# Wide operands at multiples of 128 bytes, and one DRAM tensor of x for each pair of batches

## The chip, the cores and the metric

The kernel runs on one core of one Trainium2 chip. The metric is the time of one execution on the device, in microseconds (us), as the median of several runs; lower is better.

## The reference

Inputs are q, k and v of shape [8 batches, 8 heads, 576, 64] and four weight matrices, all fp32. An attention with two sparse masks is followed by a mixer of two MLPs. Cut to what matters:

```python
scores = np.matmul(q, k.transpose(0, 1, 3, 2)) / np.sqrt(64)
rel = pos[:, None] - pos[None, :]
mask_local = (rel >= 0) & (rel < 32)                       # heads 0 to 3
mask_strided = (rel >= 0) & (pos[None, :] % 32 == pos[:, None] % 32)   # heads 4 to 7
attn = softmax(np.where(mask, scores, -1e9))
x = np.matmul(attn, v)                     # heads side by side: [8, 576, 512]
xt = x.transpose(0, 2, 1)                  # [8, 512, 576]
h = np.maximum(xt @ w_tok1, 0) @ w_tok2    # 576 -> 256 -> 576
u = x + h.transpose(0, 2, 1)
out = u + np.maximum(u @ w_ch1, 0) @ w_ch2 # 512 -> 1536 -> 512
```

## The kernel before

**Number format.** Each fp32 operand of the MLPs is split into a high part of type float32r and the rest. Three matmuls (high x high, high x rest, rest x high) then stand for one. So weights have two copies (w1h and w1l, t1h and t1l, and so on), and activations too: xh and xlo, hh and hl, uh and ul, gh and gl.

**Attention.** It comes in three forms.
- *Local heads.* `local_unit` (L132) takes a pair of batches p, a pair of heads hp, and n chunks of 128 rows from chunk c0 on, out of the 2 x 576 = 1152 rows of the two batches laid end to end (nine chunks). It is a generator: each `yield` ends a stage (loads of lq, lk and lv; scores L145; transposes L163; values L173). It leaves its result in the tile lx and stores that to DRAM. A unit whose rows lie in one batch leaves in one store (L200). Batches are 4.5 chunks long, so a unit of chunks 3 to 5 straddles the two batches; it leaves in six stores of 64 rows each (L209).
- *Strided heads, batches 0 and 1.* `strided_pe` (L221) does them on TensorE: scores L233, transposes L245, values L257, stores L271. It loads eq, ek and ev (L216 to L218). Those of batch 1 run inside the MLP of batch 0, as two "lanes" (generators over the groups of rows in GS).
- *Strided heads, batches 2 to 7.* `strided` (L278) does them without TensorE: products on GpSimd (POOL, L312 and L335), sums on VectorE (DVE, L317 and L340). Its operands q, k, v and the result are tiles "sa" that share three buffers: the load of the next batch's v goes into the buffer that held this batch's result, once that has been stored. The result leaves in four stores, one for each head (L344).

**x.** The attention's result goes by way of DRAM. Before, each batch has two DRAM tensors of [576, 256]: local heads (called xl in the profile, `xd[0]`) and strided heads (xs, `xd[1]`). `load_x` (L347) reads one half of the columns of a batch back into the tile x ([128, 5 chunks, 512]) in three loads: four whole chunks (L350), and the last 64 rows twice, one copy in each half of the partitions (L352).

**Token MLP.** `tok1` (L354) splits each of the five chunks of x (cast on ScalarE, ACT, L362; rest on DVE, L365 or L368) and multiplies it with t1 (L380). `tok2` (L400) adds x, transposed on TensorE (L404), and the second product (L408, weights operand h, moving operand t2) in PSUM, and gives u. `tok2_tail` (L411, matmuls L417, weights operand t2, moving operand h) does the last 64 rows of a batch; these are kept in DRAM (`ud`) for a ninth, short pass over all batches.

**Channel MLP.** `mlp` (L515) runs over 12 blocks fc of 128 hidden features. `up_proj(fc)` is twelve matmuls of 128x512 into h (L532, weights w1, moving operand u), then a ReLU on ACT (L535) and the rest gl on DVE (L536). `down_proj(fc)` is twelve matmuls into four accumulators (L545, weights w2, moving operand g). The order is up 0, up 1, then up fc+2 and down fc in turn. After each block stands a *step* `done()`; the 24 steps of a batch are numbered 0 to 23, and `at(i, f)` puts work of other parts into step i. So TensorE always has work of the channel MLP of batch b, and the attention and the token MLP of later batches lie between its blocks:

- step 0: `tok2_tail` of batch b;
- steps 12 and 13 (b = 0 and 1) or 11 and 11 (later): `load_half` issues the loads of the local and the strided half of x of batch b + 1;
- steps 15 to 19 or 14 to 19: one chunk of `tok1` of batch b + 1 each; steps 20 to 23: its `tok2`;
- steps 1 to 12 of batch 0 (with a last call at 13): the lanes of batch 1's strided heads; steps 0 to 15 of batch 0: splitting of weights (`do_pieces`, L82 to L112);
- the table UNITS gives the steps of the stages of the local units of later batches; `some_strided` spreads the GpSimd form over the steps from 16 of batch 0 on.

**Order.** On TensorE, VectorE, ScalarE and GpSimd the instructions run in the order in which the code writes them (`manual_schedule`). All DMAs that matter here are issued by SyncE (SP), one queue, in an order that the scheduler sets from its own simulated timeline; an issue that has to wait (for its data or a free buffer) holds up those behind it.

**Places in SBUF.** Tiles are placed one after the other. The weights come first, then a small constant tile "below" (a bias for L96; [128, 16] fp32, so 64 bytes a partition, of which one column is used, L439), then x, h, xh, xlo, uh, ul, gh, gl, ot and others. The sizes of all of these, except "below", are multiples of 128 bytes. Tiles of the later local units are placed from the other end.

Of the kernel before, what the change touches and what calls it, by code (L numbers as in the profile page):

```python
# [10 lines left out]
F32 = mybir.dt.float32  # L11
# [8 lines left out]
B, H, S, D = 8, 8, 576, 64  # L20
HL = 4
ST = 32
DM = H * D
DT = 256
DF = 1536
P = 128
# [7 lines left out]
NSB = 2  # L34
# [3 lines left out]
NSC = 5  # L38
# [14 lines left out]
def attn_mixer_kernel(ctx, tc, qT, kT, vw, qs, ks, vs, qsT, ksT, vsP, mask, mask2, w1, w2, wt1, wt2, outT):  # L53
    nc = tc.nc

    const = ctx.enter_context(tc.tile_pool(name="const", bufs=1))
    dram = ctx.enter_context(tc.tile_pool(name="dram", bufs=1, space=bass.MemoryType.DRAM))
# [18 lines left out]

    ud = [dram.tile([TAIL, DM], F32, name=f"u{b}") for b in range(B)]

    xd = [[dram.tile([S, HL * D], F32, name=f"x{m}{b}") for b in range(B)] for m in "ls"]


    def convert(stage, srcs, n):  # L82
# [49 lines left out]
    def local_unit(pool, ps_t, p, hp, c0, n, into=None, single=()):  # L132
# [9 lines left out]
        for t in range(4 * n):  # L142
            c, a = divmod(t, 4)
# [26 lines left out]
        for t in range(4 * n):  # L170
            c, a = divmod(t, 4)
# [17 lines left out]
        if nd:  # L189
            x = x_t[:, nd].rearrange("p j d -> p (j d)")  # L190
            for r in range(2):
                nc.sync.dma_start(out=into[64 * r:64 * r + 64, NSC - 1, cs], in_=x[:64])
            nc.sync.dma_start(out=xd[0][1][:64, cs], in_=x[64:])
            return
        xa, xb = xd[0][2 * p], xd[0][2 * p + 1]
        s0 = P * c0
        if s0 >= S or s0 + P * n <= S:
            x = xa if s0 < S else xb
            s0 %= S
            nc.sync.dma_start(  # L200
                out=x[s0:s0 + P * n, cs].rearrange("(c p) d -> p c d", p=P), in_=x_t[:, :n].rearrange("p c j d -> p c (j d)"))
        else:

            for c in range(n):
                for r in range(0, P, 64):
                    t = s0 + P * c + r
                    x = xa if t < S else xb
                    t %= S
                    nc.sync.dma_start(out=x[t:t + 64, cs], in_=x_t[r:r + 64, c].rearrange("p j d -> p (j d)"))  # L209


    def strided_load(pool, b, hp):
# [8 lines left out]
    def strided_pe(pool, ps_t, b, hp, j, gs, loaded, outs):  # L221
        js = slice(64 * j, 64 * j + 64)
        q_t, k_t, v_t = loaded
        n = len(gs)
# [41 lines left out]
            nc.vector.tensor_scalar_mul(x_t[:r, nf, j], av[:r, D * nf:D * nf + D], z_t[:r, nf:n])  # L266
        if j == 1:

            to = xd[1][b][:, P * hp:P * hp + P].rearrange("(j r) d -> r j d", r=ST)
            for i, g in enumerate(gs):  # L270
                nc.sync.dma_start(out=to[RG * g:RG * g + rows[i] // NJ], in_=x_t[:rows[i], i].rearrange("p j d -> p (j d)"))  # L271
        yield
# [5 lines left out]
    def strided(pool, b):  # L278
# [62 lines left out]

        yield from rows(av, av_sum)
        for h in range(HL):
            nc.sync.dma_start(out=xd[1][b][:, D * h:D * h + D].rearrange("(j r) c -> r j c", r=ST), in_=o_t[ST * h:ST * h + ST])  # L344


    def load_x(x_t, b, half):  # L347
        cs = slice(HL * D * half, HL * D * half + HL * D)
        src = xd[half][b]
        nc.sync.dma_start(out=x_t[:, :NSC - 1, cs], in_=src[:P * (NSC - 1)].rearrange("(c p) d -> p c d", p=P))  # L350
        for r in range(2):
            nc.sync.dma_start(out=x_t[64 * r:64 * r + 64, NSC - 1, cs], in_=src[P * (NSC - 1):])  # L352

    def tok1(pool, ps_t, x_t, h, cs):  # L354

# [34 lines left out]
    def new_h(pool):  # L390
        return [[pool.tile([P, DM], F32R, name=f"h{k}{m}", bufs=1) for k in "hl"] for m in range(2)]
# [44 lines left out]
    rests = [stage.tile([P, DM], U32, name=f"w_rest{i}", bufs=1) for i in range(2)]  # L436
    for t in rests:
        nc.gpsimd.memset(t, 0)
    below = const.tile([P, 16], F32, name="below")[:, :1]  # L439
    nc.gpsimd.memset(below, -15.5 / 32)  # L440
    xp = ctx.enter_context(tc.tile_pool(name="xp", bufs=2))
    up0 = ctx.enter_context(tc.tile_pool(name="up0", bufs=1))
# [24 lines left out]
    with tc.tile_pool(name="first", bufs=2) as first, \  # L467
# [22 lines left out]
        run(*loc[:2], *st[:4])  # L490
        load_t1()
        run(*loc[2:], *st[4:])
        load_x(x_t, 0, 1)
        run(tok1(xp, ps_m, x_t, h, slice(0, HL * D)))
        load_t2()
        u = [tok2(up0, ps_m, x_t, h, cc) for cc in (0, 1)]
# [134 lines left out]
    for b in range(B):  # L631
        after = {}

        def at(i, f, *args):
            after.setdefault(i, []).append(lambda: f(*args))

        def load_next(b):
            x_t = xp.tile([P, NSC, DM], F32, name="x", bufs=1)
            x_next.update(x=x_t, h=new_h(xp), u=[])
            x_next["tok1"] = tok1(xp, ps_t, x_t, x_next["h"], slice(0, DM))  # L640

        def load_half(b, half):
            assert half == 0 or turn["batch"] > b or b < NSB, (b, turn)
            load_x(x_next["x"], b, half)

        def do_tok1():
            next(x_next["tok1"], None)
# [6 lines left out]

        at(0, tok2_tail, ps_t, x_t, h, b)
        if b + 1 < B:

            local, stride, steps = (12, 13, (15, 16, 17, 18, 19, 19)) if b < 2 else (11, 11, range(14, 20))
            at(min(local, stride), load_next, b + 1)
            at(local, load_half, b + 1, 0)  # L660
            at(stride, load_half, b + 1, 1)
            for i in steps:
                at(i, do_tok1)
            for cc in range(NCC):
                at(20 + cc, do_tok2, cc)
        else:
            x_next.update(x=xp.tile([P, NSC, DM], F32, name="x", bufs=1), u=[])
            at(1, lambda: load_tails(x_next["x"]))
            for cc in range(NCC):
                at(20 + cc, do_tail, cc)  # L670
        if b == 0:
            for i in range(16):
                at(i, do_pieces, 1)
            for i in range(1, 14):
                for g in lanes:
                    at(i, next, g, None)
            at(13, first_ends)
            at(15, staging_ends)
        else:
            for i, which in zip(UNITS[b], todo[NU[b - 1]:NU[b]], strict=True):  # L680
                for j in i:
                    at(j, unit, *which)
# [77 lines left out]
```

## Time and profile before

| What | Value |
|---|---|
| Time, median of 3 runs | 859.39 us (859.14 to 860.33) |
| The profiled execution's own time | 864.13 us |
| Its span, first to last instruction | 862.4 us |
| Mean granted TensorE clock | 0.971 |
| TensorE matmul (PE) busy | 823.6 us (95%), 5804 instructions |
| TensorE weight loads (PEld) busy | 659.9 us (77%) |
| VectorE (DVE) busy | 455.9 us (53%) |
| ScalarE (ACT) busy | 257.3 us (30%) |
| GpSimd (POOL) busy | 408.4 us (47%) |
| Moved by DMA | 80.25 MB, 93 GB/s on average |

How to read the lines shown below. The *windows* list one stretch of time a line: from and to in us, its length, then busy time and number of instructions of PE, PEld, DVE, ACT and POOL, then the granted TensorE clock, the mean busy share of the 16 DMA engines, and GB/s. A row of the *timeline* has its start in us, its duration, engine, line, operation, output and inputs, with shapes (128*128 128x512 is a weights operand of 128 x 128 and a moving operand of 128 x 512), and x6 where six are taken together; in brackets, where shown, the time that the engine stood idle before it and what ended this. DMA issues are rows of SPq. A row of the *chain of waits* (the work that ended last, followed back and printed in order of time) has start, length, engine or "DMA", tile and line. L12 is line 12 of the kernel.

### The profile page before, as it was taken

To read this page: it belongs to the slowest core of one execution; us is meant where nothing else is said; L and a number is where in the kernel's file an instruction comes from. 1 tells how busy PE (TensorE), PEld (TensorE's weight loads), DVE (VectorE), ACT (ScalarE), POOL (GpSimd) and SP (SyncE) were. 2 spreads that over 40 slices of the span, in tenths; PEclk is the share of its full clock that TensorE was granted. 3 is DMA by queue.
4 is the path that set the end of the run, shared out by engine and by line. 5 is a ranking of instruction groups with operands and counts; after the bars stand their busy time and mean duration, and the time that the engine had idled before them with its cause. 6 is when DMAs were issued, how large, how long until landed. Compare 5 with 4: busy or idle time off the path is not lost.

```text
span 862.4 us, 14809 instructions
## 1 busy us (share of the span) xinstructions
PE 823.6 (95%) x5804; PEld 659.9 (77%) x5804; DVE 455.9 (53%) x1111; ACT 257.3 (30%) x722; POOL 408.4 (47%) x298
## 2 busy tenths in 40 slices
PE   5779999999979999999999999999999999999997
PEld 4657777887768777887788778877887888888885
DVE  2764555676656758575776576667652123113111
ACT  4894676323212232223222312132212111111110
POOL 0340235766874968476966695668860002002000
PEclk9559999999989999999999999999999999999999
DMA  8654744224530254024401720162013002001002
GB/s 252 218 182 146 235 151 152 114 74 123 129 89 29 90 153 145 28 74 123 144 28 64 195 82 28 56 188 69 1 55 98 1 1 82 23 1 50 1 0 49
DMA packets 67202, 80.25 MB, mean 93 GB/s; under 512 B 23364, under 2 KB 50884, under 8 KB 67132
## 3 DMA queue, kind: packets, MB, share of 16 engines
q1 hardware_dynamic: 67132, 79.30, 30.9%
q8 instruction: 46, 0.75, 0.4%
q14 instruction: 24, 0.20, 0.1%
HBM read 59.81 MB, written 19.33 MB: 92 GB/s over the span
## 4 chain that ended last, share of the span: by engine, by line
PE 84%; ACT 6%; DMA 5%; DVE 3%; issue 1%; SPq 1%; DVEq 0%
PE h L532 33%; PE acc L545 32%; PE t L380 6%; PE t L408 5%; PE t L404 2%; PE t L145 2%; PE t L173 2%; DMA x<-xs 1%; PE t L417 1%; DMA w_raw<-in_wt 1%; ACT w_rest L96 1%; ACT es L239 1%; DVE w_f L100 1%; ACT w_f L99 1%; PE t L257 1%
## 5 line engine op out<-in xcount | busy, mean ns | idle before, releaser
L335 POOL TENSOR_TENSOR sprod<-sa,ss 128x576 f32<-128x576 f32 (+8 forms) x108 | 154.6, 1463 | 89.2 <-issue 46.7
L536 DVE SCALAR_TENSOR_TENSOR gl<-h,gh 128x512 fp32r<-128x512 f32 x108 | 74.6, 691 | 231.2 <-ACT gh L535 231.1
L312 POOL TENSOR_TENSOR sprod<-sa 128x576 f32<-128x576 f32 (+8 forms) x108 | 162.7, 1536 | 51.2 <-DVE ss L317 31.3
L545 PE MATMUL acc<-gh,w2h 128*128 128x512 f32 x432 | 173.4, 401 | 0.0
L532 PE MATMUL h<-uh,w1h 128*128 128x512 f32 x432 | 171.8, 398 | 0.0
L545 PE MATMUL acc<-gh,w2l 128*128 128x512 f32 x432 | 170.1, 394 | 0.0
L532 PE MATMUL h<-uh,w1l 128*128 128x512 f32 x432 | 169.7, 393 | 0.0
L545 PE MATMUL acc<-gl,w2h 128*128 128x512 f32 x432 | 169.7, 393 | 0.0
L532 PE MATMUL h<-ul,w1h 128*128 128x512 f32 x432 | 169.3, 392 | 0.1
L535 ACT ACTIVATE gh<-h 128x512 fp32r<-128x512 f32 x108 | 64.6, 598 | 324.2 <-PE h L532 324.2
L549 POOL TENSOR_TENSOR ot<-uh,ul 128x512 f32<-128x512 f32 x36 | 50.6, 1415 | 138.0 <-DMA out_t<-ot 138.0
L545 PEld LDWEIGHTS acc<-gh,w2h 128*128 128x128 f32 x432 | 81.6, 189 | 18.8
L545 PEld LDWEIGHTS acc<-gh,w2l 128*128 128x128 f32 x432 | 81.4, 188 | 18.0
L532 PEld LDWEIGHTS h<-uh,w1h 128*128 128x128 f32 x432 | 81.2, 188 | 18.2
L545 PEld LDWEIGHTS acc<-gl,w2h 128*128 128x128 f32 x432 | 81.6, 189 | 16.9
L532 PEld LDWEIGHTS h<-ul,w1h 128*128 128x128 f32 x432 | 81.2, 188 | 17.5 <-DVE ul L397 0.5
L532 PEld LDWEIGHTS h<-uh,w1l 128*128 128x128 f32 x432 | 81.1, 188 | 17.5
L340 DVE TENSOR_REDUCE sa<-sprod 128x64 f32<-128x576 f32 (+8 forms) x108 | 79.4, 775 | 3.3 <-POOL sprod L335 3.2
L317 DVE TENSOR_REDUCE ss<-sprod 128x9 f32<-128x576 f32 (+8 forms) x108 | 79.3, 774 | 2.1 <-POOL sprod L312 1.9
L157 ACT ACTIVATE ls<-ls,lm 128x64 f32<-128x64 f32 x144 | 48.2, 336 | 34.8 <-DVE lm L154 34.8
L397 DVE TENSOR_TENSOR ul<-t,uh 128x512 fp32r<-128x512 f32 x36 | 24.8, 690 | 55.0 <-ACT uh L396 55.0
L396 ACT CAST uh<-t 128x512 fp32r<-128x512 f32 x36 | 21.1, 587 | 102.2 <-PE t L408 94.3
(91 smaller groups left out, 950.3 us busy)
## 6 DMA issues: line engine op xcount, KB each, us to landing
w_raw<-in_w SPq DMA_DIRECT2D x24, 512.0 KB
out_t<-ot SPq DMA_DIRECT2D x36, 256.0 KB
lv<-in_vw SPq DMA_DIRECT2D x20, 384.0 KB
lk<-in_kT SPq DMA_DIRECT2D x20, 208.0 KB
x<-xs SPq DMA_DIRECT2D x8, 512.0 KB
lq<-in_qT SPq DMA_DIRECT2D x20, 192.0 KB
x<-xl SPq DMA_DIRECT2D x7, 512.0 KB
sa<-in_qs SPq DMA_DIRECT2D x6, 576.0 KB
```

What stands on the lines that cost most here:

```text
L157: nc.scalar.activation(out=s_t[:, c, j, :], in_=s_t[:, c, j, :], func=AF.Exp, bias=m_t[:, c, j:j + 1], scale=-1.0, accum_out=z_t[:, c, j:j ...
L312: nc.gpsimd.tensor_tensor(out=pr.rearrange("p (n d) -> p n d", d=D), in0=k_t[:, :n, :], in1=q_t[:, i:i + 1, :].to_broadcast([P, n, D]), op ...
L317: nc.vector.tensor_reduce(out=s_t[:, i, :i + 1], in_=pr.rearrange("p (n d) -> p n d", d=D), axis=AX.X, op=ALU.add)
L335: nc.gpsimd.tensor_tensor(out=pr.rearrange("p (d n) -> p d n", n=n), in0=v_t[:, :, :n], in1=s_t[:, i:i + 1, :n].to_broadcast([P, D, n]), o ...
L340: nc.vector.tensor_reduce(out=o_t[:, i], in_=pr.rearrange("p (d n) -> p d n", n=i + 1), axis=AX.X, op=ALU.add)
L380: nc.tensor.matmul(ph[m], l[:, c, ms], r, start=(c == 0 and k == 0), stop=(c == NSC - 1 and k == 1))
L408: nc.tensor.matmul(pu, l[:, cs], r[:, m, :MAIN], start=False, stop=(m == 1 and k == 2), skip_group_check=True)
L532: nc.tensor.matmul(ph, l[:, cc, fs], r, start=(cc == 0 and k == 0), stop=(cc == NCC - 1 and k == 2))
L535: nc.scalar.activation(out=gh, in_=ph, func=AF.Relu)
L536: nc.vector.scalar_tensor_tensor(out=gl, in0=ph, scalar=0.0, in1=gh.bitcast(F32), op0=ALU.max, op1=ALU.subtract)
L545: nc.tensor.matmul(acc[cc], l[:, fc, cs], r, start=(fc == 0 and k == 0), stop=(fc == NFC - 1 and k == 2))
L549: nc.gpsimd.tensor_tensor(out=o_t, in0=uh.bitcast(F32), in1=ul.bitcast(F32), op=ALU.add)
```

## The change

It has four parts.

1. The tile "below" becomes [128, 32]: 128 bytes a partition instead of 64. All tiles placed behind it on its side move by 64 bytes, so that x, h, xh, xlo, uh, ul, gh and gl lie at multiples of 128.
2. x in DRAM becomes one tensor of [1152, 512] for each pair of batches. A local unit writes chunks of 1152 rows, so each leaves in one store, also the one that straddles two batches. The strided heads write to the same tensor, right half of the columns, in the same number of stores.
3. `load_x` takes any columns. From batch 1 on it reads all 512 at once: one load of four chunks, and one load of the last 64 rows, whose source is read twice by a broadcast over two. These are two loads of x for a batch instead of six.
4. Steps: x of the next batch is loaded at step 12 in all batches (before: 12 and 13, or 11 and 11). The lanes of batch 1's strided heads run at steps 0 to 11 instead of 1 to 12, and end at step 12 instead of 13.

```diff
--- before.py
+++ after.py
@@ -76,7 +76,10 @@
 
     ud = [dram.tile([TAIL, DM], F32, name=f"u{b}") for b in range(B)]
 
-    xd = [[dram.tile([S, HL * D], F32, name=f"x{m}{b}") for b in range(B)] for m in "ls"]
+    xd = [dram.tile([2 * S, DM], F32, name=f"x{p}") for p in range(B // 2)]
+
+    def x_strided(b, c0, n):
+        return xd[b // 2][S * (b % 2):S * (b % 2) + S, HL * D + c0:HL * D + c0 + n]
 
 
     def convert(stage, srcs, n):
@@ -190,23 +193,10 @@
             x = x_t[:, nd].rearrange("p j d -> p (j d)")
             for r in range(2):
                 nc.sync.dma_start(out=into[64 * r:64 * r + 64, NSC - 1, cs], in_=x[:64])
-            nc.sync.dma_start(out=xd[0][1][:64, cs], in_=x[64:])
+            nc.sync.dma_start(out=xd[0][S:S + 64, cs], in_=x[64:])
             return
-        xa, xb = xd[0][2 * p], xd[0][2 * p + 1]
-        s0 = P * c0
-        if s0 >= S or s0 + P * n <= S:
-            x = xa if s0 < S else xb
-            s0 %= S
-            nc.sync.dma_start(
-                out=x[s0:s0 + P * n, cs].rearrange("(c p) d -> p c d", p=P), in_=x_t[:, :n].rearrange("p c j d -> p c (j d)"))
-        else:
-
-            for c in range(n):
-                for r in range(0, P, 64):
-                    t = s0 + P * c + r
-                    x = xa if t < S else xb
-                    t %= S
-                    nc.sync.dma_start(out=x[t:t + 64, cs], in_=x_t[r:r + 64, c].rearrange("p j d -> p (j d)"))
+        nc.sync.dma_start(
+            out=xd[p][P * c0:P * (c0 + n), cs].rearrange("(c p) d -> p c d", p=P), in_=x_t[:, :n].rearrange("p c j d -> p c (j d)"))
 
 
     def strided_load(pool, b, hp):
@@ -266,7 +256,7 @@
             nc.vector.tensor_scalar_mul(x_t[:r, nf, j], av[:r, D * nf:D * nf + D], z_t[:r, nf:n])
         if j == 1:
 
-            to = xd[1][b][:, P * hp:P * hp + P].rearrange("(j r) d -> r j d", r=ST)
+            to = x_strided(b, P * hp, P).rearrange("(j r) d -> r j d", r=ST)
             for i, g in enumerate(gs):
                 nc.sync.dma_start(out=to[RG * g:RG * g + rows[i] // NJ], in_=x_t[:rows[i], i].rearrange("p j d -> p (j d)"))
         yield
@@ -341,15 +331,14 @@
 
         yield from rows(av, av_sum)
         for h in range(HL):
-            nc.sync.dma_start(out=xd[1][b][:, D * h:D * h + D].rearrange("(j r) c -> r j c", r=ST), in_=o_t[ST * h:ST * h + ST])
-
-
-    def load_x(x_t, b, half):
-        cs = slice(HL * D * half, HL * D * half + HL * D)
-        src = xd[half][b]
+            nc.sync.dma_start(out=x_strided(b, D * h, D).rearrange("(j r) c -> r j c", r=ST), in_=o_t[ST * h:ST * h + ST])
+
+
+    def load_x(x_t, b, cs):
+        src = xd[b // 2][S * (b % 2):S * (b % 2) + S, cs]
         nc.sync.dma_start(out=x_t[:, :NSC - 1, cs], in_=src[:P * (NSC - 1)].rearrange("(c p) d -> p c d", p=P))
-        for r in range(2):
-            nc.sync.dma_start(out=x_t[64 * r:64 * r + 64, NSC - 1, cs], in_=src[P * (NSC - 1):])
+
+        nc.sync.dma_start(out=x_t[:, NSC - 1, cs], in_=src[P * (NSC - 1):].unsqueeze(0).to_broadcast([2, 64, cs.stop - cs.start]))
 
     def tok1(pool, ps_t, x_t, h, cs):
 
@@ -436,7 +425,7 @@
     rests = [stage.tile([P, DM], U32, name=f"w_rest{i}", bufs=1) for i in range(2)]
     for t in rests:
         nc.gpsimd.memset(t, 0)
-    below = const.tile([P, 16], F32, name="below")[:, :1]
+    below = const.tile([P, 32], F32, name="below")[:, :1]
     nc.gpsimd.memset(below, -15.5 / 32)
     xp = ctx.enter_context(tc.tile_pool(name="xp", bufs=2))
     up0 = ctx.enter_context(tc.tile_pool(name="up0", bufs=1))
@@ -490,7 +479,7 @@
         run(*loc[:2], *st[:4])
         load_t1()
         run(*loc[2:], *st[4:])
-        load_x(x_t, 0, 1)
+        load_x(x_t, 0, slice(HL * D, DM))
         run(tok1(xp, ps_m, x_t, h, slice(0, HL * D)))
         load_t2()
         u = [tok2(up0, ps_m, x_t, h, cc) for cc in (0, 1)]
@@ -637,11 +626,10 @@
         def load_next(b):
             x_t = xp.tile([P, NSC, DM], F32, name="x", bufs=1)
             x_next.update(x=x_t, h=new_h(xp), u=[])
+            assert turn["batch"] > b or b < NSB, (b, turn)
+            load_x(x_t, b, slice(0, DM))
             x_next["tok1"] = tok1(xp, ps_t, x_t, x_next["h"], slice(0, DM))
 
-        def load_half(b, half):
-            assert half == 0 or turn["batch"] > b or b < NSB, (b, turn)
-            load_x(x_next["x"], b, half)
 
         def do_tok1():
             next(x_next["tok1"], None)
@@ -654,11 +642,8 @@
 
         at(0, tok2_tail, ps_t, x_t, h, b)
         if b + 1 < B:
-
-            local, stride, steps = (12, 13, (15, 16, 17, 18, 19, 19)) if b < 2 else (11, 11, range(14, 20))
-            at(min(local, stride), load_next, b + 1)
-            at(local, load_half, b + 1, 0)
-            at(stride, load_half, b + 1, 1)
+            at(12, load_next, b + 1)
+            steps = (15, 16, 17, 18, 19, 19) if b < 2 else range(14, 20)
             for i in steps:
                 at(i, do_tok1)
             for cc in range(NCC):
@@ -671,10 +656,10 @@
         if b == 0:
             for i in range(16):
                 at(i, do_pieces, 1)
-            for i in range(1, 14):
+            for i in range(12):
                 for g in lanes:
                     at(i, next, g, None)
-            at(13, first_ends)
+            at(12, first_ends)
             at(15, staging_ends)
         else:
             for i, which in zip(UNITS[b], todo[NU[b - 1]:NU[b]], strict=True):
```

## The prediction

> **What bounds it now.** I read the page's totals and its chain first, then the windows, then the chain in order of time where TensorE's clock falls, and last the issuing queue (SP) there.
>
> ```profile
> PE 823.6 (95%) x5804; PEld 659.9 (77%) x5804; DVE 455.9 (53%) x1111; ACT 257.3 (30%) x722; POOL 408.4 (47%) x298
> ...
> PE 84%; ACT 6%; DMA 5%; DVE 3%; issue 1%; SPq 1%; DVEq 0%
> ```
>
> TensorE is the bound, and 84% of the chain is its own work. So the change can pay in two ways only: fewer ns per matmul, or less waiting for loads (DMA, 5%). The waits stand in two stretches.
>
> ```profile
> 145.00:160.00 15.00, 13.37 (x58) 10.43 (x57) 7.86 (x10) 5.90 (x10) 9.93 (x8) 1.00 0.71 256
> ...
> 234.00:255.00 21.00, 16.37 (x60) 12.60 (x59) 9.78 (x13) 2.84 (x5) 17.75 (x14) 0.84 0.46 117
> ```
>
> ```profile
> 149.24 0.62 ACT L362 CAST xh<-x 128x512 fp32r<-128x512 f32 x1 [2.94 <-DMA x<-xs]
> ...
> 149.91 0.50 PE L380 MATMUL t<-xh,t1h 128*128 128x512 f32 x1 [1.41 <-ACT xh L362]
> ```
>
> ```profile
> 246.71 0.80 PE L380 MATMUL t<-xh,t1h 128*128 128x512 f32 x1 [4.63 <-ACT xh L362]
> ```
>
> ```profile
> 234.38 3.44 DMA xs<-sa
> 238.40 7.62 DMA x<-xs
> 246.71 3.23 PE t L380 x6
> 249.94 4.05 PE acc L545 x12
> 255.36 2.75 PE h L532 x12
> ```
>
> Both are the first tok1 step of a batch, late because x has not landed. For batch 1 TensorE waits 1.41 us and keeps its clock (1.00). For batch 2 it waits 4.63 us and the granted clock falls to 0.84 in that window: six matmuls take 3.23 us and twelve 4.05, where twelve take 2.75 at full clock. That is (3.23 - 1.37) + (4.05 - 2.75) = 3.2 us more. Batch 2's late load costs 4.6 + 3.2 = 7.8 us in all.
>
> **Batch 2's load: the single store.** What the queue did ahead of it:
>
> ```profile
> 203.45 0.38 SPq L200 DMA_DIRECT2D xl<-lx  x1
> ...
> 228.91 3.65 SPq L209 DMA_DIRECT2D xl<-lx  x6
> 232.65 2.64 SPq L344 DMA_DIRECT2D xs<-sa  x4
> 235.40 1.10 SPq L350 DMA_DIRECT2D x<-xl  x1
> ...
> 237.91 0.45 SPq L285 DMA_DIRECT2D sa<-in_vs  x1
> 238.40 0.43 SPq L350 DMA_DIRECT2D x<-xs  x1
> ```
>
> ```profile
> 228.80 1.34 DVE L340 TENSOR_REDUCE sa<-sprod 128x64 f32<-128x1152 f32 x1
> ```
>
> The strided result is ready at 230.14 (228.80 + 1.34), but its four stores (L344) stand behind six pieces of a local unit that straddles the two batches, until 232.65. The new form sends a unit in one store, 0.38 us by L200's row. So the strided stores start at about 230.2, 2.45 us earlier, and the last lands at about 235.4 instead of 237.8 (234.38 + 3.44). The load of sa for batch 3 follows (it waits for the same landing), then x at about 235.9, behind it in the queue.
>
> How long the load takes is the unknown. Before, from 235.40 to 246.02, three loads moved x's local half, sa and x's strided half: 0.66 + 0.59 + 0.66 = 1.9 MB. Now x's first load (four chunks at full width, 1.05 MB) and sa must come, 1.64 MB.
>
> ```profile
> 235.00:247.00 12.00, 7.37 (x32) 5.74 (x31) 3.23 (x5) 1.56 (x3) 10.79 (x9) 0.95 0.72 192
> 322.00:332.00 10.00, 8.98 (x133) 6.89 (x132) 8.43 (x13) 2.79 (x11) 8.68 (x7) 1.00 0.93 285
> ```
>
> At the old pace it lands at 235.4 + 10.6 x 1.64/1.9 = 244.5; at the 285 GB/s that the same loads reach a batch later, at 235.9 + 5.75 = 241.7. TensorE arrives at 242.1 (246.71 - 4.63), and the cast adds 0.69. The wait becomes 0.3 to 3.1 us; I take the middle, 1.7, which is nearest to the 1.41 us that left the clock at 1.00, so the slow matmuls go as well: 4.6 - 1.7 + 3.2 = 6.1 us gained. Ends: 1.5 (a wait of 3.1 that still costs the clock) and 7.5. What is late next there is the same load, by less.
>
> **Batch 1's load, and the lanes moved a step.** The strided lanes of batch 1 run at steps 0 to 11 instead of 1 to 12, and x comes at step 12 in one piece instead of the strided half at 13.
>
> ```profile
> 86.41 0.39 SPq L217 DMA_DIRECT2D ek<-in_ksT  x1
> ...
> 88.02 0.39 PE L532 MATMUL h<-uh,w1h 128*128 128x512 f32 x1
> ...
> 90.86 1.27 PE L233 MATMUL t<-ek,eq 64*126 64x126 f32 x10
> ```
>
> ```profile
> 127.90 1.27 PE L233 MATMUL t<-ek,eq 64*126 64x126 f32 x10
> ...
> 139.24 3.87 SPq L271 DMA_DIRECT2D xs<-ex  x5
> ...
> 145.00 0.39 SPq L350 DMA_DIRECT2D x<-xs  x1
> ```
>
> The move itself has a price. The first scores (L233) now stand right after tok2_tail, where TensorE is at 88.02, in order. Their operand ek was issued at 86.41; loads and stores of its kind land 3.4 us (the L344 row of the chain) to 4.2 us after issue (x of batch 1: 145.00 to the cast at 149.24), so at 89.8 to 90.6. TensorE waits 1.8 to 2.6 us, and everything behind it on TensorE, the next up-projection first, waits too. I take 1.8, as ek is the smaller transfer; it is nothing if the queue issues the load earlier. On the other side, nine steps take 37.04 us between the two L233 rows, 4.1 each, so the last strided stores leave at 139.24 - 4.1 + 1.8 = 136.9, and x at 142.7. It holds 0.39 MB more ahead of its first use than the strided half did, 1.4 to 2.1 us at the two paces above, so it lands after 5.6 to 6.3 us, at 148.3 to 149.0. TensorE arrives at 148.5 + 1.8 less the cast, 149.6. The 1.41 us go. Sum here +1.8 - 1.4 = +0.4; ends -1.4 and +2.6.
>
> **Later batches.** From batch 3 on x moves from step 11 to 12, which costs nothing: the tightest, batch 4, is issued at 415.00 and first used at 422.77, and its six pieces shrink too. Without that cover, one step (some 3.4 us) would be the price.
>
> ```profile
> 415.00 0.38 SPq L350 DMA_DIRECT2D x<-xl  x1
> ```
>
> ```profile
> 422.77 1.13 ACT L362 CAST xh<-x 128x512 fp32r<-128x512 f32 x2
> ```
>
> **The 128-byte addresses.** The tile "below" takes 64 bytes and stands ahead of x, h, xh, uh, gh and all later tiles; its neighbours before it are multiples of 128, so those tiles lie 64 past a multiple of 128 and the weights do not. With 128 bytes all of them are at multiples.
>
> ```profile
> 719.68 1.40 PE t L408 x6
> 721.08 2.76 PE h L532 x12
> 723.84 1.37 PE t L417 x6
> ```
>
> ```profile
> 248.03 0.63 PE L380 MATMUL t<-xh,t1l 128*128 128x512 f32 x1
> ...
> 249.31 0.63 PE L380 MATMUL t<-xh,t1l 128*128 128x512 f32 x1
> ```
>
> Moving operand off, weights on (L417, L532): 228 to 230 ns. Moving operand on (t2), weights off (h): 233 ns (L408). No row has both on. That the weights' offset is what costs is the plain reading, and 8 x 24 matmuls of L408 then win 4.5 ns each, 0.9 us. I take this and no change elsewhere. The bounds: that on is the slow place for the moving operand, +4.5 ns for each of the 2836 others (2592 of L532 and L545, 196 of L380, 48 of L417), +12.8 us; that it is faster by as much, -12.8; and at most the half of the 427 ns that the same matmul takes at half clock (three from 248.03 to 249.31), 213.5, so -43 us.
>
> [...]
>
> **Sum.** -6.1 + 0.4 - 0.9 = -6.6 us. The profiled execution took 864.13 us, so 857.5 for it; the median shown, 859.39, lies 4.7 below, so 852.8.
>
> **The rivals.** (1) The address of the moving operand matters and on is better: 852.8 - 12.8 = 840, or down to 809. For it: 229 stands above half of 427. Against it: L408, moving operand on, isn't fast.
> (2) Slower: on is the slow place, by the same rows read the other way: L408 is the only line with its moving operand on, and the slowest. 852.8 + 0.9 + 12.8 = 866.5. It decides from 2.3 ns a matmul (6.6/2836).
> (3) The load doesn't come earlier: the queue puts other loads ahead, or the pace stays. Then 7.8 and 1.4 us stay and 1.8 and -0.9 come: 860.3.
> (4) The last chunk. It now comes in one load whose source is twice the same 64 rows, where two loads of 64 rows stood. If such a load ran on two of 16 engines, its 256 KB would take 0.131 MB an engine:
>
> ```profile
> 85.00:95.00 10.00, 9.94 (x47) 7.58 (x46) 6.20 (x20) 6.00 (x14) 1.96 (x2) 1.00 0.84 264
> ```
>
> 264 GB/s at a share of 0.84 is 19.6 GB/s for a busy engine, so 6.7 us instead of 0.8. But the last chunk's cast comes at 259.52, 13.5 us after the first:
>
> ```profile
> 246.04 0.62 ACT L362 CAST xh<-x 128x512 fp32r<-128x512 f32 x1 [8.82 <-DMA x<-xs]
> ```
>
> ```profile
> 259.52 0.62 ACT L362 CAST xh<-x 128x512 fp32r<-128x512 f32 x1 [0.77 <-PE t L380]
> ```
>
> So it is hidden unless it is later than that; with loads queued behind it on those engines I give 1 us for each of seven batches and half of the gain: 863.
>
> [...] No view quoted here counts engines.
>
> **Chances.** The forecast 0.47, its own range 849 to 858 (the ends of the terms); (1) 0.15 for 840 and 0.08 for the floor; (2) 0.10; (3) 0.15; (4) 0.05. A measurement of this kernel can tell 0.2%, 1.7 us, from no change. Faster: nearly all of the forecast and (1), a little of (3), 0.70; same: most of (3), 0.12; slower: (2), (4), some of (3), 0.18. The range leaves out the floor and (2): 839.5 to 861.
>
> **What would show it.** After: one store for each unit and none of 64 rows; strided stores for batch 2 right behind the strided result; x of batch 2 issued near 236 and TensorE's wait there under 3 us, with the clock of 234 to 255 back to 1.00; a new wait of about 2 us ahead of the first L233 of the main loop; L408 at 229 ns. Wrong would be: L532 in groups of twelve at anything but 2.75 us (then the addresses decide), or a wait of 4 us at batch 2 as before.

## The result, and the profile after

The changed kernel takes 868.29 us (median of 4 runs, 867.43 to 870.44) where the kernel before takes 859.86 in the same series (859.14 to 861.28): ratio 1.010, interval 1.0077 to 1.0123, 8.4 us slower. The forecast was 852.8.

The totals and the chain of the page after:

```profile
span 868.7 us, 14705 instructions
...
PE 831.8 (96%) x5804; PEld 661.8 (76%) x5804; DVE 453.4 (52%) x1111; ACT 257.6 (30%) x722; POOL 407.1 (47%) x298
...
PE 84%; DMA 7%; ACT 5%; DVE 2%; issue 1%; SPq 1%; DVEq 0%
```

TensorE executes the same 5804 instructions, and is busy 8.2 us longer (831.8 against 823.6; 823.6 again in a second execution of the kernel before). The waits for loads did not go either: DMA has 7% of the chain where it had 5%.

First the matmuls, in the chain in order of time, where nothing but the channel MLP runs:

```profile
728.68 1.40 PE t L406 x6
730.08 5.60 PE h L521 x24
735.68 2.80 PE acc L534 x12
738.48 2.80 PE h L521 x12
```

L521 and L534 are the former L532 and L545. Twelve took 2.75 us and take 2.80: 229 and 233 ns a matmul. L406 (before L417) went from 1.37 to 1.40 us for six. L397 (before L408), the one line for which the forecast had a gain, is nearly unchanged at 1.38 to 1.40.

Then TensorE's waits, in its timeline; the brackets show idle time and what ended it:

```profile
87.51 1.24 PE L223 MATMUL t<-ek,eq 64*126 64x126 f32 x10 [1.75 <-DMA ek<-in_ksT]
...
148.37 0.50 PE L369 MATMUL t<-xh,t1h 128*128 128x512 f32 x1 [1.38 <-ACT xh L351]
...
243.68 0.80 PE L369 MATMUL t<-xh,t1h 128*128 128x512 f32 x1 [2.20 <-ACT xh L351]
...
335.91 0.51 PE L369 MATMUL t<-xlo,t1h 128*128 128x512 f32 x1 [1.62 <-DVE xlo L357]
...
426.52 0.50 PE L369 MATMUL t<-xlo,t1h 128*128 128x512 f32 x1 [1.96 <-DVE xlo L357]
```

The wait for ek is new, as forecast. Batch 1's wait (before 1.41) stays. Batch 2's falls from 4.63 to 2.20. Two waits for xlo follow, at the tok1 of batches 3 and 4; the first is new, the second was 0.99. In the windows of batches 2 and 4 the clock falls below 1:

```profile
234.00:255.00 21.00, 18.80 (x75) 14.60 (x74) 11.82 (x14) 4.06 (x7) 17.36 (x13) 0.92 0.27 91
420.00:430.00 10.00, 8.04 (x31) 6.15 (x30) 7.54 (x6) 2.25 (x4) 8.05 (x6) 0.89 0.03 12
```

Batch 2's load in SP's queue, and in the chain (with batch 1's load, at 140.54):

```profile
228.01 0.38 SPq L198 DMA_DIRECT2D x<-lx  x1
229.26 2.39 SPq L334 DMA_DIRECT2D x<-sa  x4
233.94 0.35 SPq L275 DMA_DIRECT2D sa<-in_vs  x1
234.40 0.68 SPq L339 DMA_DIRECT2D x<-x  x1
235.13 0.56 SPq L341 DMA_DIRECT2D x<-x  x1
```

```profile
140.54 7.14 DMA x<-x
...
234.40 8.59 DMA x<-x
243.01 0.63 ACT xh L351
243.68 3.23 PE t L369 x6
246.91 2.85 PE acc L534 x12
```

The unit leaves in one store, the strided stores stand right behind it, and x is issued 5.2 us after the strided result (229.24), where it was 8.3 us before (230.14 to 238.40): 3.1 us won. But it lands at 243.0: 8.59 us for a load of full width, against 7.62 for half of the columns.

The wait for xlo at batch 3 begins on VectorE, in its timeline after:

```profile
332.70 0.62 DVE L187 TENSOR_TENSOR lx<-t,lz 128x192 f32<-128x192 f32 x2 [5.11 <-DMA x<-lx]
```

VectorE waits 5.11 us until the former store of lx has landed, as lx has one buffer there; gl and xlo stand behind it in order. The same row of the kernel before:

```profile
333.66 0.62 DVE L184 TENSOR_TENSOR lx<-t,lz 128x192 f32<-128x192 f32 x2 [1.44 <-DMA xl<-lx]
```

That store was issued at 324.52, behind x, its last chunk and a load of lv:

```profile
319.23 0.38 SPq L339 DMA_DIRECT2D x<-x  x1
319.65 0.53 SPq L341 DMA_DIRECT2D x<-x  x1
323.32 0.33 SPq L142 DMA_DIRECT2D lv<-in_vw  x1
324.52 0.38 SPq L198 DMA_DIRECT2D x<-lx  x1
```

In the semaphore events of the trace, the load of the four chunks has sixteen increments between 4.8 and 8.2 us after the end of its issue. The load of the last chunk has one early, at 0.4 us, and two late ones, 10.4 and 10.9 us after, and the store behind it has fourteen up to 4.4 us and two at 6.9 and 7.7. The packets of the same trace fit this. Those of 2 KB (640 in all, 512 rows of the four chunks and 128 of the last) run from 327.35 us on in two rows, with one every 0.08 us in each, and from 329.94 to 330.71 in one. Of the store's 384 packets 336 start by 328.85, and the last 48, an eighth, not before 330.89. An eighth is two of sixteen engines: that two engines were late with the last chunk, and therefore with the store queued behind it, is an estimate from these numbers, as no record names an engine.

### The profile page after: what moved, and what is told of

Its sections match the earlier page's. It is cut to its first block, busy times and chain, and to the rows that moved or that the text cites. A ratio compares the mean times of both kernels' runs of the same rounds, so it can differ in the third digit from the quotient of the medians.

```text
span 868.7 us, 14705 instructions
## 1 busy us (share of the span) xinstructions
PE 831.8 (96%) x5804; PEld 661.8 (76%) x5804; DVE 453.4 (52%) x1111; ACT 257.6 (30%) x722; POOL 407.1 (47%) x298
## 4 chain that ended last, share of the span: by engine, by line
PE 84%; DMA 7%; ACT 5%; DVE 2%; issue 1%; SPq 1%; DVEq 0%
PE h L521 33%; PE acc L534 32%; PE t L369 6%; PE t L397 5%; DMA x<-x 2%; PE t L393 2%; PE t L148 2%; PE t L176 1%; DMA w_raw<-in_wt 1%; ACT w_rest L99 1%; PE t L406 1%; DMA x<-lx 1%; PE t L247 1%; ACT ls L160 1%; ACT w_f L102 1%
## 5 line engine op out<-in xcount | busy, mean ns | idle before, releaser
L521 PE MATMUL h<-uh,w1h 128*128 128x512 f32 x432 | 174.1, 403 | 0.0
L534 PE MATMUL acc<-gh,w2h 128*128 128x512 f32 x432 | 174.0, 403 | 0.0
L521 PE MATMUL h<-ul,w1h 128*128 128x512 f32 x432 | 171.3, 396 | 0.1
L521 PE MATMUL h<-uh,w1l 128*128 128x512 f32 x432 | 171.1, 396 | 0.0
L534 PE MATMUL acc<-gh,w2l 128*128 128x512 f32 x432 | 170.5, 395 | 0.0
L534 PE MATMUL acc<-gl,w2h 128*128 128x512 f32 x432 | 170.3, 394 | 0.0
L521 PEld LDWEIGHTS h<-uh,w1h 128*128 128x128 f32 x432 | 81.7, 189 | 19.6
L534 PEld LDWEIGHTS acc<-gh,w2h 128*128 128x128 f32 x432 | 81.4, 189 | 19.7
L521 PEld LDWEIGHTS h<-uh,w1l 128*128 128x128 f32 x432 | 81.7, 189 | 19.4
L534 PEld LDWEIGHTS acc<-gh,w2l 128*128 128x128 f32 x432 | 81.2, 188 | 19.3
L521 PEld LDWEIGHTS h<-ul,w1h 128*128 128x128 f32 x432 | 81.7, 189 | 18.5 <-DVE ul L386 0.5
L534 PEld LDWEIGHTS acc<-gl,w2h 128*128 128x128 f32 x432 | 81.4, 188 | 17.9
```

What stands on the lines that cost most here:

```text
L521: nc.tensor.matmul(ph, l[:, cc, fs], r, start=(cc == 0 and k == 0), stop=(cc == NCC - 1 and k == 2))
L534: nc.tensor.matmul(acc[cc], l[:, fc, cs], r, start=(fc == 0 and k == 0), stop=(fc == NFC - 1 and k == 2))
```

## Experiments: the addresses

Four theories were at hand for the 2.80 us: the place of the moving operand, the distance between the two operands, the execution (a rate that differs from one execution to the next), and no cost at all (the time lost to transfers alone). Each experiment is the kernel before (or the one named) with the edit shown. "Ratio" is against the kernel before, timed in the same series, with its 95% interval. Line numbers differ by a few from kernel to kernel; the tiles tell which operation a row is.

**The address change alone, and all the rest alone.**

```diff
-    below = const.tile([P, 16], F32, name="below")[:, :1]
+    below = const.tile([P, 32], F32, name="below")[:, :1]
```

The addresses alone (e1):

> The kernel before with the tile below at 128 bytes and nothing else, so that only addresses differ. If a moving operand at a multiple of 128 costs 4.3 ns more for each matmul of 512 columns (12 matmuls of L532 took 2.75 us before and 2.80 us in the changed kernel), 2836 matmuls give +12.2 us: 872. If the address costs nothing and the changed kernel lost its time by its transfers: 859.9.

All the rest alone (e2):

> The changed kernel with the tile below back at 64 bytes: everything but the addresses. If the addresses cost 12.2 us and add up with the rest: 868.3 - 12.2 = 856.1, twelve matmuls back at 2.75 us. If the addresses cost nothing: 868.3.

Measured: the addresses alone 867.43 us where the kernel before takes 863.32 in this series, ratio 1.0053 (1.0038 to 1.0068), 4.6 us, twelve matmuls in 2.80. The rest alone 867.57 us, ratio 1.0053 (1.0024 to 1.0082), twelve in 2.75. The addresses cost time, and the rest, forecast at -5.7 us, costs time as well: no single part explains the result.

**Which address.** The weights start at byte 2944 of the built program, which is 384 modulo 512. The traces hold no addresses; the argument needs only the distances, which follow from the sizes of the tiles. The slices of the weights that the matmuls load lie whole multiples of 512 bytes apart. Pads ahead of the weights and ahead of x move the two separately.

```diff
+    const.tile([P, 16], F32, name="pad")    # e3, e5: 64 bytes; e9: 32 columns, 128 bytes
     w1h = const.tile([P, NCC, DF], F32R, name="w1h")
...
-    below = const.tile([P, 16], F32, name="below")[:, :1]
+    below = const.tile([P, 32], F32, name="below")[:, :1]   # e3; e4: 24, e6: 48, e15: 8, e16: 112 columns
```

In e10 the line of "below", with 16 columns, stands ahead of w1h, and nothing behind the weights.

e3:

> The kernel before with 64 bytes ahead of the weights and the tile below at 128 bytes: weights and activations all lie 64 past a multiple of 128. If only the moving operand's address counts: L532 and L545 stay at 2.75 us for twelve, L408 falls from 1.40 to 1.37 us for six (its moving operand t2 now at 64): 859.0. If the two operands must lie 64 apart (weights at a multiple, moving operand off it): twelve in 2.80 us, 872.

e4:

> The kernel before with the tile below at 96 bytes: activations lie 96 past a multiple of 128, weights at multiples. If any place off a multiple of 128 is as good as 64: 859.9, twelve matmuls in 2.75 us. If only multiples of 64 off 128 are good, or a place between gives more or fewer pieces per row: another time for twelve, 2.80 us (872) or above.

e5:

> The kernel before with 64 bytes ahead of the weights: weights lie 64 past a multiple of 128, x, u and g at multiples. So far twelve matmuls took 2.75 us only with weights at a multiple and the moving operand 64 past it, and 2.80 us at (0, 0), (64, 64) and (0, 96). If that one pairing is the fast one: L532 and L545 2.80 us for twelve, L408 (weights h at a multiple, moving t2 64 past it) falls from 1.40 to 1.37 us for six, total as with the address change alone, ratio 1.005. If any two places 64 apart are fast: twelve in 2.75 us, L408 1.37, ratio 0.999. If the rate belongs to the execution and not to the addresses: any of these.

e6:

> The kernel before with the tile below at 192 bytes: weights at multiples of 128, moving operand 64 past, but 128 bytes further than before. If the pairing modulo 128 decides: twelve matmuls in 2.75 us, L408 1.40 for six, ratio 1.000. If the rate belongs to the execution or to a larger period of addresses: 2.80 us, ratio 1.005 or more.

e9:

> The kernel before with 128 bytes ahead of the weights, so that all tiles move by 128: weights begin at 3072 (0 modulo 512) and the moving operands stay 64 behind them modulo 512. So far twelve matmuls took 2.75 us where the moving operand lies 64 past the weights modulo 512 (wherever the pair lies), and 2.80 at distances of 96, 128 and 192. If the distance decides: 2.75 us for twelve, L408 1.40 for six, the time of before (ratio 1.000, or 0.996 as with the pair moved by 64). If the places themselves decide, or the rate belongs to the execution: 2.80 may come, ratio 1.005 or more.

e10:

> The kernel before with the tile below placed ahead of the weights: the moving operands keep their addresses to the byte, the weights move by 64, distance 0 modulo 512. If the moving operand's own address decides: 2.75 us for twelve. If the distance decides, any rate but unchanged addresses of x, u and g: 2.80 us if only 64 is good (ratio 1.005 to 1.01), 2.75 if all up to 64 are.

e15:

> The kernel before with the tile below at 32 bytes: moving operands 32 past the weights modulo 512. If the cost grows with the distance up to about 100: between 2.72 and 2.75 us for twelve, ratio 0.995 to 1.000. If only multiples of 64 are good: 2.80 us, ratio 1.005 to 1.01.

e16:

> The kernel before with the tile below at 448 bytes: moving operands 448 past (64 short of) the weights modulo 512. L408, whose moving operand lay so, took 1.40 us for six. If the sign of the distance counts: 2.80 us for twelve, ratio 1.005 to 1.01, and L408 (now the other way round, t2 64 past h) falls to 1.37. If only the size of the distance counts: 2.75 us, ratio 1.000, and L408 stays.

e12, the kernel before, again:

> The kernel before, unchanged, as a second execution with a profile. Where the rate belongs to the addresses: 2.75 us for twelve matmuls of L532 and L545 again. Where it belongs to the execution it may be 2.80. Ratio 1.000. It also shows how much of TensorE's waits (1.41 us at batch 1, 4.63 at batch 2) and of the clock in the first 80 us differs between executions of one kernel.

| Kernel | weights, bytes mod 512 | moving operand (u, g, h, xh), mod 512 | distance mod 512 | twelve matmuls, us | ratio to before |
|---|---|---|---|---|---|
| e10 | 448 | 448 | 0 | 2.72 | 0.9947 (0.9928 to 0.9966) |
| e15 | 384 | 416 | 32 | 2.80 | 1.0118 (1.0092 to 1.0144) |
| before again (e12) | 384 | 448 | 64 | 2.75 | 0.9999 (0.9981 to 1.0017) |
| e5 | 448 | 0 | 64 | 2.75 | 0.9956 (0.9936 to 0.9975) |
| e9 | 0 | 64 | 64 | 2.75 | 1.0042 (1.0022 to 1.0061) |
| e4 | 384 | 480 | 96 | 2.80 | 1.0102 (1.0072 to 1.0133) |
| e1 (as changed) | 384 | 0 | 128 | 2.80 | 1.0053 (1.0038 to 1.0068) |
| e3 | 448 | 64 | 128 | 2.80 | 1.0068 (1.0050 to 1.0085) |
| e6 | 384 | 64 | 192 | 2.80 | 1.0109 (1.0082 to 1.0136) |
| e16 | 384 | 320 | 448 | 2.80 | 1.0136 (1.0109 to 1.0163) |

(e3's groups lie between 2.78 and 2.80.) The rows behind the table are the chain in order of time; of e10 (distance 0), e5 (64) and e15 (32):

```profile
726.17 2.72 PE h L532 x12
728.89 2.72 PE acc L545 x12
```

```profile
740.26 2.75 PE h L533 x12
743.00 2.75 PE acc L546 x12
```

```profile
743.50 2.80 PE h L532 x12
746.30 2.80 PE acc L545 x12
```

What follows. e10 has u, g and h at the same bytes as the kernel before and is faster; e5 and e1 have them at the same bytes (0 modulo 512) and differ; so do e9 and e6 (64). So the place of the moving operand is not what counts, and a multiple of 128 is neither good nor bad. For the matmuls of L532 and L545 the distance to the weights orders all ten kernels: 0 gives 227 ns a matmul, 64 gives 229, and 32, 96, 128, 192 and 448 give 233. Repeated executions of one kernel gave the same rate (the kernel before twice), so it is not the execution. 256 wasn't tried, so that the period may be 256. Why the distance counts, no run shows.

L408 does not follow, so the distance is not shown to be a rule for every matmul: six took 1.38 to 1.41 us in all of these, also at a distance of 0 (e10). This stays open.

The cost. 2836 matmuls by (2.80 - 2.75)/12 us are 11.8 us. The six kernels at 2.80 (e1, e3, e4, e6, e15, e16) have a mean ratio of 1.0098, 8.4 us, and each between 4.6 and 11.7. The three at distance 64 have a mean of 0.9999, but lie apart by 0.4% to both sides, so that one such kernel's ratio says less than its interval does; a part of it stands in the waits of tok1, below.

## Experiments: the store, the loads and the lanes

All with "below" at 64 bytes, so at 2.75 us for twelve, except the last three (e13, e17, e18), which have it ahead of the weights and take 2.72.

**One store for each unit, and nothing else** (e14: one DRAM tensor for a pair, x still in halves at steps 12 and 13, or 11 and 11, the lanes at steps 1 to 12).

```diff
+        nc.sync.dma_start(
+            out=xd[p][P * c0:P * (c0 + n), cs].rearrange("(c p) d -> p c d", p=P), in_=x_t[:, :n].rearrange("p c j d -> p c (j d)"))
...
+    def load_x(x_t, b, cs):
+        src = xd[b // 2][S * (b % 2):S * (b % 2) + S, cs]
...
         for r in range(2):
             nc.sync.dma_start(out=x_t[64 * r:64 * r + 64, NSC - 1, cs], in_=src[P * (NSC - 1):])
```

> The kernel before with one DRAM tensor of x for each pair of batches and one store for each unit, and nothing else: x in halves at the same steps, the lanes at steps 1 to 12, addresses as before. If the six stores are what makes x of batch 2 late: the strided stores go out 2.4 us earlier, TensorE's wait at batch 2 (4.1 to 4.6 us in the kernel before) falls to about 2, the clock there rises, ratio 0.993 to 0.996. If the pace of the DMA engines sets the landing and not the queue: the wait stays above 3.5 us, ratio 1.000.

Measured: 857.97 us, ratio 0.9972 (0.9953 to 0.9992), 2.4 us won by the ratio, less than expected. Its chain at batch 2:

```profile
228.27 0.34 SPq L334
...
234.91 5.05 DMA x<-x
239.99 0.63 ACT xh L352
240.64 1.88 DVE xlo L358
```

The strided stores go out right behind the strided result and x lands at 240.0; TensorE waits 1.25 us for xh. This step of the forecast works. But the rest of x, xlo, takes VectorE 1.88 us, against a median of 0.70 in the kernel before, and TensorE waits 1.40 us for that. The six stores were worth 2.4 us, not 6.1.

**The last chunk in two loads** (e7: the changed kernel, with "below" at 64 bytes).

```diff
-        nc.sync.dma_start(out=x_t[:, NSC - 1, cs], in_=src[P * (NSC - 1):].unsqueeze(0).to_broadcast([2, 64, cs.stop - cs.start]))
+        for r in range(2):
+            nc.sync.dma_start(out=x_t[64 * r:64 * r + 64, NSC - 1, cs], in_=src[P * (NSC - 1):])
```

> The changed kernel with below at 64 bytes, and the last 64 rows of x read by two loads of 64 rows instead of one broadcast load. If that one load runs on two DMA engines and holds up what is queued behind it there: its landing falls from 10.9 us to under 6, the store of lx behind it lands in about 4 us instead of 7.7, VectorE's wait for it falls from 4.9 to about 1.4 us, the stall of TensorE near 335 us (1.36) goes, and the time falls by 1 to 4 us against the same kernel with the broadcast load. If the width of the load is not what delays the store: no change.

Measured: 866.21 us, ratio 1.0031 (1.0010 to 1.0053), against 1.0053 with the broadcast: about 1.9 us, inside the intervals of the two, and from two series. What the trace shows is plainer. VectorE's row:

```profile
331.56 0.62 DVE L187 TENSOR_TENSOR lx<-t,lz 128x192 f32<-128x192 f32 x2 [2.85 <-DMA x<-lx]
```

The wait falls from 4.89 us (the same kernel with the broadcast) to 2.85, the two loads land within 7.8 us (of the end of their issue), the store behind them in 5.1, and TensorE's wait near 335 (1.36 us) is gone. The direction is as expected, but each of the three stays above its expected value (about 1.4, under 6, about 4).

**Two chunks a load** (e8).

```diff
-        nc.sync.dma_start(out=x_t[:, :NSC - 1, cs], in_=src[:P * (NSC - 1)].rearrange("(c p) d -> p c d", p=P))
+        for c in range(0, NSC - 1, 2):
+            nc.sync.dma_start(out=x_t[:, c:c + 2, cs], in_=src[P * c:P * c + 2 * P].rearrange("(c p) d -> p c d", p=P))
```

> As the kernel with two loads for the last rows, and the four whole chunks of x in two loads of two chunks, so that the first step of tok1, which needs chunks 0 and 1 only, waits for half as much. If the size ahead of the first use is what makes TensorE wait: the stall at batch 1 (1.4 to 1.7 us) goes, that at batch 2 (0.7 to 2.2 us) goes too: 2 to 4 us less than without. If the latency or what stands ahead in the queue sets it: no change.

Measured in the same series: 859.32 us, ratio 0.9959 (0.9934 to 0.9984) against 1.0031: 6.2 us by the ratios, 6.9 by the medians, where 2 to 4 were expected. TensorE's rows with one load of four chunks, and with two of two:

```profile
151.12 0.80 PE L370 MATMUL t<-xh,t1h 128*128 128x512 f32 x1 [2.66 <-ACT xh L352]
...
245.96 0.49 PE L370 MATMUL t<-xh,t1h 128*128 128x512 f32 x1 [1.41 <-ACT xh L352]
```

```profile
149.67 0.50 PE L371 MATMUL t<-xh,t1h 128*128 128x512 f32 x1 [0.94 <-ACT xh L353]
...
241.78 0.40 PE L371 MATMUL t<-xh,t1h 128*128 128x512 f32 x1
```

2.66 and 1.41 us become 0.94 and nothing, 3.1 us of the gain; the rest is not accounted for row by row. What stands in one transfer with the first use counts here; a load of all columns of four chunks makes tok1's first step wait for chunks that it does not read.

**The lanes** (e11). With the loads of two chunks, the lanes back at steps 1 to 12 and x of batch 1 at step 13:

```diff
-            at(12, load_next, b + 1)
+            at(13 if b == 0 else 12, load_next, b + 1)
...
-            for i in range(12):
+            for i in range(1, 14):
...
-            at(12, first_ends)
+            at(13, first_ends)
```

> The kernel with x in loads of two chunks (two loads for the last rows, below at 64 bytes), with the lanes back at steps 1 to 12 and x of batch 1 loaded at step 13. If the move of the lanes costs the wait for ek: the wait of 1.5 to 2.7 us ahead of the first L223 goes, TensorE's wait at batch 1 stays near 1 us as only half of x has to land, and the time falls by 1.5 to 2.5 us against the same kernel with the lanes early. If x lands a step later instead: the wait at batch 1 grows by as much and nothing is won.

857.74 us, ratio 0.9961 (0.9937 to 0.9986): no other than with the lanes early, but in another series. So both were run once more in one series, with "below" ahead of the weights (early e17, late e18).

> The fastest kernel so far with the lanes at steps 0 to 11 and x of batch 1 loaded at step 12. If the wait for ek is lost time: 2 to 3 us slower than with the lanes back. If it only takes the place of a wait for x at batch 1: the same within 1 us.

> The fastest kernel so far (distance 0, x in loads of two chunks, lanes at steps 1 to 12), again: ratio 0.990.

Early: 853.74 us, ratio 0.9909 (0.9882 to 0.9937). Late: 849.98, ratio 0.9872 (0.9844 to 0.9900). The early lanes cost 3.8 us by the medians and 3.2 by the ratios; the two intervals just overlap, and at 2.75 us for twelve no cost was seen (e8 and e11, two series). 1.5 of it is the wait for ek, in the timeline of the early one:

```profile
87.84 1.24 PE L224 MATMUL t<-ek,eq 64*126 64x126 f32 x10 [1.49 <-DMA ek<-in_ksT]
```

Another part is that its wait for xlo at batch 4 was 2.23 us, and 1.02 with the lanes late.

**The version that beats both** (e13). Distance 0, one store a unit, x in loads of two chunks and two loads of the last rows, the lanes late.

> The kernel with x in loads of two chunks and the lanes back (ratio 0.996), with below ahead of the weights (distance 0 modulo 512, ratio 0.995 when alone). If the two are independent they add: 2836 matmuls by 2.3 ns = 6.5 us less than the first, ratio 0.990, about 852. If faster matmuls only run into the waits for x sooner: some of it comes back as waits, ratio 0.992 to 0.995.

850.18 us, ratio 0.9901 (0.9867 to 0.9934); the repeat e18 is the same kernel. 0.9961 x 0.9947 = 0.9908: the parts add. In its window of batch 2 TensorE hardly waits and the clock stays at 1. Batch 4's tok1 begins at 412.64 here; its wait for xlo is still there, and the clock stays at 1 behind it:

```profile
234.00:255.00 21.00, 20.59 (x91) 16.70 (x90) 15.32 (x21) 5.29 (x9) 21.00 (x14) 1.00 0.19 61
```

```profile
414.05 0.50 PE L372 MATMUL t<-xlo,t1h 128*128 128x512 f32 x1 [1.02 <-DVE xlo L360]
```

```profile
420.00:430.00 10.00, 10.00 (x46) 8.29 (x45) 9.77 (x14) 1.95 (x4) 4.38 (x2) 1.00 0.18 59
```

## Why the prediction was wrong

The forecast was -6.6 us and +8.4 came, 15.0 us apart. Two steps failed. The addresses were put at -0.9 us and cost 4.6 alone (e1). The store, the loads and the lanes were put at -5.7 together and cost 4.6 alone (e2): the single store was sized too high, the load of full width and the early lanes too low, and the broadcast load stood in the sum at nothing. The forecast's own range has a slip as well: the ends of its terms add up to 849.6 and 859.6, not 849 to 858.

**The addresses: the first step that failed.** The reading of the rows was "that the weights' offset is what costs is the plain reading", with -0.9 us. Two lines differed in both operands' places (L532: weights on a multiple, moving operand 64 past; L408: the reverse), and the prediction took one operand for the cause. The sign of rival (2), "on is the slow place", came true with twelve matmuls at 2.80 us, its price of +12.8 us is near the 11.8 by the rows and above the 8.4 measured, but its mechanism is not right either: in e5 the moving operand is on a multiple and fast. Neither rival allowed for the distance of the two. Given 0.10, it was left out of the range. That its 866.5 us comes so near the 868.29 measured is luck: it reckons with transfers that win 5.7 us, and they cost 4.6.

**The second step, batch 2's load: right mechanism, wrong size.** The strided stores go out right behind the strided result and x 5.2 us after it (forecast 5.8). But the load took 8.59 us; the forecast's ends were 5.8 and 8.6, and the middle was taken. The wait is 2.20 us (1.7), and here the step failed that let the slow matmuls go at such a wait: six still took 3.23 us. What came is 4.63 - 2.20 of the wait and 4.05 - 2.85 for the next twelve, 3.6 us instead of 6.1. The single store alone won 2.4 (e14). That 1.41 us left the clock alone was one row; 2.20 did not. Nor does the length of the wait decide it alone: in e4 TensorE waits longer at the same place and the clock of 234 to 255 is 1.00.

```profile
242.75 0.50 PE L380 MATMUL t<-xh,t1h 128*128 128x512 f32 x1 [3.06 <-ACT xh L362]
```

**Batch 1 and the lanes.** The new wait for ek is 1.75 us, forecast 1.8. The other half failed: the 1.41 us did not go (1.38). The chain gives x 7.14 us to land where 5.6 to 6.3 were expected, and TensorE reached the step 61.2 us after it came to the wait for ek (85.76 to 146.99) where 62.3 were reckoned (88.02 to 148.5, and 1.8); the runs give no reason for the second. The early lanes cost 3.2 to 3.8 us in the one pair timed together, e17 and e18, where +0.4 was forecast and +2.6 was the upper end.

**Rival (4), given 0.05, came true as a mechanism** (at the end the rows of x go two at a time, and a store behind them is held up; the two engines were a supposition), by another victim than the one looked for. The prediction followed the last chunk itself, which is in time; who is late is the store of lx queued behind it, and through the single buffer of lx VectorE, and through its order xlo. The wait at batch 3 is 1.62 us, and e2 has 1.36 of it where e7, without the broadcast, has none; by the times of these two it costs about 1.9 us. A shorter wait there comes without the broadcast too (0.63 us in e1), so the 1.62 is not the broadcast's alone.

**What nobody had in the sum: batch 4's wait for xlo.** Before 0.99 us, after 1.96, and then the clock falls to 0.89. xlo itself is long, 2.63 us before and 3.66 after, against a median of 0.70 and 0.69 over all 36 of each, in a stretch where GpSimd multiplies without a break (four products in 5.61 us). VectorE's xlo and the operation behind GpSimd's products, before and after:

```profile
423.51 2.63 DVE L368 TENSOR_TENSOR xlo<-x,xh 128x512 fp32r<-128x512 f32 x1
...
425.56 1.73 POOL L549 TENSOR_TENSOR ot<-uh,ul 128x512 f32<-128x512 f32 x1
```

```profile
422.81 3.66 DVE L357 TENSOR_TENSOR xlo<-x,xh 128x512 fp32r<-128x512 f32 x1
...
424.64 1.28 POOL L538 TENSOR_TENSOR ot<-uh,ul 128x512 f32<-128x512 f32 x1
```

Before, xlo ends 0.5 us after the last product, and ot is the longer one. After, ot takes 1.28 (its median is 1.29), and xlo ends 0.5 us after ot. All twenty profiled executions show one or the other: xlo of 2.4 to 2.6 us with ot of 1.73 to 1.77 and a wait of TensorE of 0.7 to 1.0, or 3.6 to 3.9 with 1.25 to 1.31 and a wait of 1.9 to 2.2. That VectorE and GpSimd hold each other up here is the author's reading of these rows; no run took GpSimd's products away, so it isn't shown. Which goes first is worth about 1.2 us, an estimate from the middles of the two groups of waits. The long form came in the changed kernel, e2 to e4, e6 to e9, e16 and e17, the short one in the kernel before (both times) and the others; what decides between them is open. Behind the long form the clock fell in the changed kernel, e2, e8, e9 and e17, and not in e3, e4, e6, e7 and e16. This is likely one source of the spread at distance 64, where e9 has the long form and e5 and e12 the short one.

**The ledger.** One store -2.4 (e14, 0.9972); from there full-width loads and early lanes +5.1 (e7, 1.0031); the broadcast +1.9 (e2, 1.0053). These add up to e2's +4.6 by construction, as each is the difference of two neighbours; they come from three series, and by the intervals each difference is uncertain by an estimated 2 to 3 us. The lanes are 3.2 to 3.8 of it in the last pair and nothing in the other. The addresses are +4.6 alone (e1), +8.4 in the mean of six. With e2's they give 9.1 and 13.0, and 8.4 was measured (6.6 to 10.6): the first is within the intervals, the second is above. That a slower TensorE comes later to the waits for x, and so waits less, fits (e1 waits 3.10 us at batch 2 where the kernel before, again, waits 4.14), but wasn't isolated.

## What to carry to other kernels

- Rows of two lines whose operands both differ can't tell which operand, or which relation between them, costs; a rival for the relation belongs beside one for each. A change of one pad in the right place tells it in a run.
- Merging transfers saves issues (two loads of x for a batch instead of six), but the first user then waits for all of the bytes in one: with one load of four chunks TensorE waited 2.66 and 1.41 us, with two loads of two 0.94 and nothing (e7, e8). What is queued behind a transfer can pay for it as well: the store of lx landed 7.7 us after the end of its issue behind the broadcast load, whose last increment came at 10.9, and 5.1 behind two loads of 64 rows (e7). Look for the next store or load, and for who waits for it.
- A step that moves earlier must be followed to its operand's load; the new wait is paid on TensorE (1.75 us for ek here), and what was to be won at the other end does not come if the load there gets longer (x of batch 1 took 7.14 us to land where 5.6 to 6.3 were expected, and the wait of 1.41 us became 1.38).

## What the runs showed of the hardware that was not expected

- The rate of the channel MLP's matmuls (128x128 by 128x512, float32r, new weights for each) goes with the distance of the two operands in SBUF, modulo 512 bytes (or 256): 227 ns at 0, 229 at 64, 233 at 32, 96, 128, 192 and 448. L408, of the same shape, did not follow: six took 1.38 to 1.41 us in all of these kernels. Placing a 64-byte tile ahead of the weights instead of behind them made this kernel 0.5% faster (0.9947).
- The granted clock of the first 83 us differed between two executions of the kernel before, with nothing changed: 0.75 in the one and 0.86 in the other, and the first matmul of tok1 stood at 36.8 and at 34.4 us. Spans of single executions are therefore not compared here, but ratios, and stretches behind that place.
